# A decode step of two attention and MLP layers on one core: moving K's transposes, the softmax maximum and P's selection in the order of work

## The chip, the core and the metric

The kernel runs on one core of a Trainium2 chip. The metric is the device time of one execution in microseconds (us); lower is better. The core has five engines that run side by side, each through its own instructions in order, and that wait for each other on semaphores: TensorE (PE; its weight loads are shown apart as PEld), VectorE (DVE), ScalarE (ACT), GpSimd (POOL) and SyncE (SP). Here SP issues every load from the chip's memory (HBM) into the on-chip memory; 16 DMA engines carry them out.

## The reference

One token goes through attention, MLP, attention, MLP. Both attentions read the same K and V caches, of which only the last 4096 positions of each of 32 heads count; both MLPs read the same weights.

```python
def _A_ref(x, k_cache, v_cache, wq, wo):          # x (1,1,640), caches (1,32,32768,192)
    B, Sq, D = x.shape
    Hq, Dh = 32, 192
    W = 4096
    q = (x @ wq).reshape(B, Sq, Hq, Dh).transpose(0, 2, 1, 3)
    k = k_cache[:, :, Sk - W:, :]
    v = v_cache[:, :, Sk - W:, :]
    scores = jnp.einsum("bhqd,bhkd->bhqk", q, k) * (Dh ** -0.5)
    p = _softmax(scores, axis=-1)
    o = jnp.einsum("bhqk,bhkd->bhqd", p, v)
    return o.transpose(0, 2, 1, 3).reshape(B, Sq, Hq * Dh) @ wo
...
x = A_x
x = x + _A_ref(_layernorm(x), A_k_cache, A_v_cache, A_wq, A_wo)
x = x + _B_ref(_layernorm(x), B_w1, B_w2, B_w3, B_w4)
x = x + _A_ref(_layernorm(x), A_k_cache, A_v_cache, A_wq, A_wo)
x = x + _B_ref(_layernorm(x), B_w1, B_w2, B_w3, B_w4)
```

With a sequence of one token, the MLP's shifted parts are zero, so that its first half adds nothing and `x + gelu(layernorm(x) @ w3) @ w4` is left. K and V of one head are 4096 x 192 numbers of 2 bytes, 1536 KB each.

## The kernel before

**Loads and cells.** On-chip memory holds 12 cells, each the size of one head's K or V. `take` (L147) hands out the cell that was given back first, `give` returns one. `stream` lists all loads in a fixed order; `need` issues the next ones in that order, on SP's queue. Each issue waits until its cell is free, that is, until the engine that last used it is done; the loads behind it on SP wait too. Issues go through eight DMA semaphores in turn, so that at most eight loads are in flight. In layer 1, heads 0 to 7 have their transposed K still in memory (`NKEEP`), and a few V's stay as well.

**Attention.** Heads go in groups of 4, 8 groups per layer; layer 0 takes the heads from 28..31 down to 0..3, layer 1 up from 0..3. While a group's probabilities are applied to V, the next group's scores are made. The steps, with their lines:

- `T(h, half)`, `transpose_quart` (L433, L450): DVE transposes K of head h in four quarters of 0.94 us each; a half is two. The last quarter gives K's cell back. In most of the kernel the transposed quarters go into an `area` of one cell that is used in turn.
- `S(h, half, ...)`, `scores` (L534): 12 matmuls on PE that add half a head's scores to `ST_ps`.
- Softmax (`softmax_steps`, L551): `part_max` (L557, DVE), `turn_max` (L562, PE), `full_max` (L567 and L572, DVE), `spread_max` (L580 on PE, then the exponential L586 on ACT), `turn_p` (L591, DVE), `swap` (L602 on PE, copy L605 on ACT, sums L607 on PE), `recip` (L614, L616, DVE).
- `pv(h)` (L648): 16 matmuls on PE, P times V; then V's cell is given back and DVE brings the result out (L655). `o_fold` (L657) sums and scales it.
- The group's output product with wo, as a row (`out_row`, L694, added on DVE by `y_ps()`, L702 and L704) or as columns (`out_proj`, L676), and the query of the group after next (`qproj_steps`: L469 or L480, `spread` L494, `repeat` L501, `block` L518).

**Order.** PE, DVE, ACT and SP run in the order in which the code emits their instructions. So the order of the calls in `attention` (L813 to L960) is the order of the work. For a group: first the head h0 and the softmax with the projections between (L850 to L889), then for each of its four heads `pv`, the scores of one more head of the next group, and the fold (L897 to L952). Temporary results of PE share two PSUM buffers (`psm`).

Three kinds of group are told apart. A plain group does this as it stands. The last group but one (`hurry`) has to finish the scores and the softmax of the last group within its own products, since the last group (`final`) has none to make. Before the change, layer 1's last group but one (`quick`) had its own order, in which K's transposes are emitted before the products, and layer 0's another one.

Of the kernel before, what the change touches and what calls it, by code (L numbers as in the profile page):

```python
# [10 lines left out]
F32 = mybir.dt.float32  # L11
# [48 lines left out]
def kernel(  # L60
# [57 lines left out]
    kl = low.tile([P, NKL * Dh], BF16, name="kl")  # L118
# [186 lines left out]
    o_words = o_sb[:].rearrange("p e c i -> p (e c i)")  # L305
# [402 lines left out]
    def turn_row(acc):  # L708
        y_ps = psm.tile([P, ND], F32, tag="psm")
        N = D // 2  # L710
        for n in range(ND):
            a, b = n * P, (n + 1) * P
            for i in range(2):
                lo_, hi = max(a, i * N), min(b, (i + 1) * N)
                if lo_ < hi:
                    nc.tensor.matmul(y_ps[lo_ - a:hi - a, n:n + 1], lhsT=acc[:, lo_ - i * N:hi - i * N],
                                     rhs=ident[0:33, 32 * i:32 * i + 1], start=True, stop=True)
        return y_ps

    def attention(layer, x_cur, rs_cur, x_new, z_new, rs_new, ss_new):  # L720
# [13 lines left out]
        def T(h, half):  # L734
            for q in (2 * half, 2 * half + 1):
                if (h, q) not in Th:
                    Th[h, q] = transpose_quart(layer, h, q)

        def S(h, half, ST_ps, hq):
            if layer == 1 and h < NKEEP:  # L740
                if half == 1:
                    scores(h, [Th.pop((h, q)) for q in range(NT)], 0, ST_ps, hq)
                    give(("T", h))
                return
            scores(h, [Th.pop((h, q)) for q in (2 * half, 2 * half + 1)], 2 * half, ST_ps, hq)
            if half == 1 and layer == 0 and h == last_plain:
                give(("area", layer))
                area[0] = None
# [52 lines left out]
        pending = None  # L801
# [11 lines left out]
        for gi, cur in enumerate(groups):  # L813
            nxt = list(enumerate(groups[gi + 1])) if gi + 1 < len(groups) else []
            hurry = gi + 2 == len(groups)
            final = gi + 1 == len(groups)

            quick = hurry and layer == 1
            ST_n = None
            if nxt:  # L820
                part_max, turn_max, full_max, spread_max, turn_p, swap, recip = softmax_steps(len(cur), ST, sc, o_words)
                ST_n = next_scores()
                if layer == 1 and gi == 0:

                    keep = [hh for hh in nxt if hh[1] < NKEEP]
                    del nxt[:len(keep)]
                    q = qproj_steps(groups[2][0] // QH, xc)
                    q1[2]()
                    q1[3]()
                    for q2, h2 in keep:  # L830
                        for half in range(2):
                            T(h2, half)
                            S(h2, half, ST_n, q2)
                        if q2 == 0:
                            v_words(1)
                    for step in (part_max, turn_max, full_max, spread_max, turn_p):
                        step()

                    need("v", 1, cur[-1] + 1)
                    q[0]()  # L840
                    PT = swap()
                    q[1]()
                    rl = recip()
                    q[2]()
                    q[3]()
                else:
                    if gi == 0:
                        for step in q1:
                            step()
                    h0 = nxt[0][1]  # L850
                    T(h0, 0)
                    part_max()
                    T(h0, 1)
                    S(h0, 0, ST_n, 0)
                    turn_max()
                    full_max()
                    S(h0, 1, ST_n, 0)
                    spread_max()
                    h1 = nxt[1][1]
                    q = None  # L860
                    if gi + 2 < len(groups):
                        q = qproj_steps(groups[gi + 2][0] // QH, xc, row=q_row if gi in rows else None)
                    if q:
                        q[0]()
                    in_row = gi - 1 in rows
                    if pending is not None:
                        y_ps = out_row(layer, *pending, acc, gi - 1 == rows[0]) if in_row else out_proj(layer, pending)
                    turn_p()
                    if quick:
                        y_ps()  # L870
                    T(h1, 0)
                    if q:
                        q[1]()
                        q[2]()
                    if in_row:
                        if not quick:
                            y_ps()
                            if gi - 1 == rows[-1]:
                                add_y(turn_row(acc), 2)
                        pending = None  # L880
                    if pending is not None:
                        add_y(y_ps, 2)
                        pending = None
                    PT = swap()
                    T(h1, 1)
                    if q:
                        q[3]()
                    rl = recip()
                    nxt.pop(0)  # L889
            else:  # L890
                PT, rl = early
            oT = short_bf16("oT", NA, 2)
            fold = None
            order = list(enumerate(cur))
            if layer == 1 and gi == 0:
                order.insert(0, order.pop(cur.index(VC)))
            for hq, h in order:  # L897
                if quick and hq == 1:
                    (q2, h2), (q3, h3) = nxt
                    T(h2, 0)  # L900
                    T(h2, 1)
                elif quick and hq == 2:
                    T(h3, 1)
                pv(layer, h, hq, PT, steps[3] if quick and hq == 3 else fold)
                if final:
                    if hq == 0:
                        add_y(out_proj(layer, pending) if layer == 0 else turn_row(acc), 1)
                    if hq == 1:
                        center_y()
                    fold = None  # L910
                    if hq < QH - 2:
                        o_fold(h, oT, rl)
                    else:
                        def fold(h=h):
                            o_fold(h, oT, rl)

                    continue
                if quick and hq == 1:
                    S(h2, 0, ST_n, q2)
                    S(h2, 1, ST_n, q2)  # L920
                    T(h3, 0)
                elif quick and hq == 2:
                    S(h3, 0, ST_n, q3)
                    o_fold(h, oT, rl)
                    S(h3, 1, ST_n, q3)
                    steps = softmax_steps(len(cur), ST_n, sc, kl[:].bitcast(F32))
                    for step in steps[:3]:
                        step()
                    continue
                elif hurry and hq == 1:  # L930
                    (q2, h2), (q3, h3) = nxt
                    for half in range(2):
                        T(h2, half)
                        S(h2, half, ST_n, q2)
                    T(h3, 0)
                    S(h3, 0, ST_n, q3)
                    T(h3, 1)
                elif hurry and hq == 2:
                    S(h3, 1, ST_n, q3)
                    steps = softmax_steps(len(cur), ST_n, sc, o_words)  # L940
                    steps[0]()
                    steps[1]()
                elif nxt and not (hurry and hq == 3):
                    q2, h2 = nxt.pop(0)
                    for half in range(2):
                        T(h2, half)
                        S(h2, half, ST_n, q2)
                o_fold(h, oT, rl, len(groups) - 4 > gi >= 2 * layer)
                if hurry and hq == 3:
                    for step in steps[4 if quick else 2:5]:  # L950
                        step()
                    early = steps[5](), steps[6]()  # L952
            if final:
                fold()
            if (layer, gi) == (1, 1):
                clear_rows()
            last = (cur[0] // QH, oT)
            if not final:
                pending = last
            ST = ST_n  # L960
# [146 lines left out]
```

## Time and profile before

| | us |
|---|---|
| median of 3 runs | 511.44 (511.27 to 511.87) |
| the profiled execution, its time | 511.84 |
| its span in the profile | 509.9 |
| DVE, transposes of K (L450), 224 of 943 ns | 200.3 busy |
| PE, scores (L534), 1536 | 157.0 busy; 101.6 idle before |
| of that idle time, ended by L450 | 69.1 |
| PE, P times V (L648) | 103.1 busy; 7.4 idle for V's landing |
| DVE, bringing the product out (L655), 64 | 37.2 busy; 110.4 idle before, for PE |
| HBM read | 214.01 MB, 420 GB/s over the span |

All of it is from one profiled execution. In groups of instructions, busy time is that of the engine on that line, and idle time is the time in which the engine had nothing to do just before it; the name behind an arrow is the instruction that ended that time. Windows give, for a stretch of the span, the busy time of each engine, the clock that TensorE was granted, the share of time in which the 16 DMA engines were moving, and GB/s. The timeline gives start and length of instructions, like ones merged, with the idle time before them in brackets. Idle time of an engine that is not the bound costs nothing.

### The profile page before, as it was taken

The page shows a single profiled execution, that of the slowest core. Times are in us where ns is not written, and L with a number is a line of the kernel's source. Part 1 is how long each engine was busy: PE and PEld are TensorE (multiplying, and loading weights), DVE is VectorE, ACT ScalarE, POOL GpSimd, SP SyncE. Part 2 cuts the span into 40 slices and gives each one's busy share as a digit, 9 for nine tenths or more (in the row PEclk, how much of TensorE's full clock was granted, in tenths as well). Part 3 has the DMA queues.
Part 4 walks back from the last instruction along what each step waited for, and adds up shares of the span by engine and source line. Part 5 has one row for each costly group of instructions (what it writes and reads, how often), then busy time and mean ns, then how long its engine had stood idle before and what let it go on. Part 6 is the DMA issues. An engine that isn't in the chain of part 4 may idle for free.

```text
span 509.9 us, 9485 instructions
## 1 busy us (share of the span) xinstructions
PE 328.0 (64%) x4084; PEld 190.0 (37%) x4084; DVE 292.0 (57%) x604; ACT 48.9 (10%) x173; POOL 3.7 (1%) x16
## 2 busy tenths in 40 slices
PE   1057667677586675866665766658656765758685
PEld 0024333333343342533333643435333442434354
DVE  2077557657666656467624244756576566767522
ACT  1000101010010100101010100001010100101111
POOL 2000000000000000000000000000000000000000
PEclk9996666765756667577665585666786577886655
DMA  8999999999999999999999999999999999999996
GB/s 370 432 432 429 438 433 432 429 433 423 419 423 445 432 418 449 428 404 459 429 392 414 377 439 424 435 429 437 429 422 437 432 422 433 426 433 429 419 408 242
DMA packets 12015, 214.63 MB, mean 421 GB/s; under 512 B 2565, under 2 KB 3077, under 8 KB 7429
## 3 DMA queue, kind: packets, MB, share of 16 engines
q1 hardware_dynamic: 11972, 214.02, 98.5%
q8 instruction: 32, 0.52, 0.4%
q14 instruction: 11, 0.08, 0.0%
HBM read 214.01 MB, written 0.00 MB: 420 GB/s over the span
## 4 chain that ended last, share of the span: by engine, by line
DMA 42%; PE 28%; DVE 24%; issue 4%; ACT 1%; SPq 1%; DVEq 0%; ACTq 0%
DMA cell<-in_A_k_cache_dram 24%; DVE cell L450 17%; DMA cell<-in_A_v_cache_dram 14%; PE ST_ps L534 11%; PE O_ps L648 9%; DMA cell<-in_B_w_dram 4%; DVE o_sb L655 2%; PE qr_ps L469 2%; PE nb_ps L580 1%; PE yr_ps L694 1%; DVE words L557 1%; DVE o_sb L591 1%; PE l_ps L607 1%; PE y_ps L1051 1%; PE PT_ps L602 1%
## 5 line engine op out<-in xcount | busy, mean ns | idle before, releaser
L534 PE MATMUL ST_ps<-cell,Qblk 128*16 128x256 bf16 x1536 | 157.0, 364 | 101.6 <-DVE cell L450 69.1
L450 DVE STREAM_TRANSPOSE cell<-cell 128x768 uint32<-128x768 uint32 x224 | 200.3, 943 | 5.8 <-DMA cell<-in_A_k_cache_dram 5.4
L534 PEld LDWEIGHTS <-Qblk 128*16 128x16 bf16 x1536 | 82.8, 108 | 170.8 <-issue 146.9
L648 PE MATMUL O_ps<-cell,PT 128*2 128x384 bf16 x1000 | 103.1, 482 | 9.3 <-DMA cell<-in_A_v_cache_dram 7.4
L655 DVE STREAM_TRANSPOSE o_sb<-O_ps 128x384 f32<-128x384 f32 x64 | 37.2, 581 | 110.4 <-PE O_ps L648 110.3
L648 PEld LDWEIGHTS <-PT 128*2 128x2 bf16 x1024 | 46.1, 102 | 24.7 <-issue 15.7
L591 DVE STREAM_TRANSPOSE o_sb<-o_sb 128x256 bf16<-128x256 bf16 x15 | 6.7, 445 | 33.1 <-ACT o_sb L586 26.1
L663 ACT ACTIVATE words<-oT_ps,words 32x6 bf16<-32x6 f32 x40 | 10.3, 257 | 159.5 <-PE oT_ps L662 148.5
L662 PE MATMUL oT_ps<-o_sb,Lq 128*32 128x6 f32 x160 | 13.8, 195 | 10.4 <-DVE o_sb L655 9.8
L662 PEld LDWEIGHTS oT_ps<-o_sb,Lq 128*32 128x32 f32 x160 | 12.6, 143 | 20.4 <-issue 15.1
L668 ACT ACTIVATE words<-oT_ps,words 32x6 bf16<-32x6 f32 x24 | 6.2, 257 | 111.8 <-PE ST_ps L534 96.3
L480 PE MATMUL qT_ps<-words,wq_sb 128*128 128x1 bf16 x210 | 7.1, 165 | 12.8 <-DMA wq_sb<-in_A_wq_dram 11.9
L694 PE MATMUL yr_ps<-cell,words 128*1 128x320 bf16 x108 | 14.8, 439 | 0.0
L469 PE MATMUL qr_ps<-wq_sb,words 128*1 128x384 bf16 x90 | 14.2, 471 | 0.0
L494 DVE TENSOR_TENSOR o_sb<-qT_ps,words 128x24 bf16<-128x24 f32 (+1 forms) x18 | 3.0, 166 | 18.9 <-PE qT_ps L480 17.1
L480 PEld LDWEIGHTS <-wq_sb 128*128 128x128 bf16 x210 | 6.7, 102 | 14.0 <-DMA wq_sb<-in_A_wq_dram 13.0
L602 PE MATMUL PT_ps<-o_sb,ident 128*32 128x32 bf16 x240 | 6.8, 237 | 7.7 <-DVE o_sb L591 2.6
L607 PE MATMUL l_ps<-o_sb,words 128*128 128x4 f32 x30 | 7.8, 331 | 5.3 <-ACT PT L605 5.3
L602 PEld LDWEIGHTS <-ident 128*32 128x32 bf16 x256 | 5.6, 113 | 14.4 <-issue 14.1
L583 ACT COPY o_sb<-nb_ps 128x1 f32<-128x1 f32 x15 | 2.4, 159 | 88.6 <-PE nb_ps L580 88.6
L667 PE MATMUL oT_ps<-o_sb,Lq 128*32 128x6 f32 x48 | 6.0, 199 | 6.1 <-DVE o_sb L666 6.1
L667 PEld LDWEIGHTS oT_ps<-o_sb,Lq 128*32 128x32 f32 x48 | 5.7, 142 | 10.4 <-issue 9.9
(153 smaller groups left out, 202.0 us busy)
## 6 DMA issues: line engine op xcount, KB each, us to landing
cell<-in_A_k_cache_dram SPq DMA_DIRECT2D x56, 1536.0 KB, 25.6
cell<-in_A_v_cache_dram SPq DMA_DIRECT2D x56, 1536.0 KB, 26.3
cell<-in_A_wo_dram SPq DMA_DIRECT2D x13, 960.0 KB, 23.1
wq_sb<-in_A_wq_dram SPq DMA_DIRECT2D x5, 1536.0 KB, 13.4
cell<-in_A_v_cache_dram SPq DMA_DIRECT2D x6, 768.0 KB, 23.7
cell<-in_B_w_dram SPq DMA_DIRECT2D x1, 1536.0 KB, 11.8
cell<-in_B_w_dram SPq DMA_DIRECT2D x2, 768.0 KB, 10.3
cell<-in_A_wo_dram SPq DMA_DIRECT2D x3, 480.0 KB, 17.0
```

Of the source, the lines that this page charges most:

```text
L450: nc.vector.transpose(Tu, Ku[:, :, q * NY:(q + 1) * NY])
L469: nc.tensor.matmul(qr_ps[32 * i:32 * i + 1, :], lhsT=xc[:, kc:kc + 1], rhs=wq_sb[:, kc, t0 * P + i * N:t0 * P + (i + 1) * N], start=(kc == ...
L480: nc.tensor.matmul(qT_ps[:, tl:tl + 1], lhsT=wq_sb[:, kc, t * P:(t + 1) * P], rhs=xc[:, kc:kc + 1], start=(kc == 0), stop=(kc == ND - 1))
L534: nc.tensor.matmul(ST_ps[r:r + QW, :].rearrange("p (g i) -> p g i", g=ng), lhsT=Q[n], rhs=T4[:, :, f, :, t], start=(hq == 0 and n == 0), s ...
L591: nc.vector.transpose(held["PrT"], held["Pr"])
L602: nc.tensor.matmul(PT_ps[32 * m:32 * (m + 1), :, :, ng * q:ng * (q + 1)], lhsT=Eq[:, q, :], rhs=src[:, m:QW:NM], start=True, stop=True)
L607: nc.tensor.matmul(l_ps[:], lhsT=ones, rhs=held["lh"][:], start=True, stop=True)
L648: nc.tensor.matmul(O_ps[r:r + 2, :], lhsT=PT[:, hq, 2 * i:2 * i + 2], rhs=v_pair(V, h, 2 * i * Dh, 2 * Dh), start=(i < 4), stop=(i >= NB - 4))
L655: nc.vector.transpose(o_sb[:], O_ps.rearrange("p (e a c) -> p e c a", e=2, c=NA))
L662: nc.tensor.matmul(oT_ps[r, :], lhsT=Lq[:], rhs=o_sb[:, e, :, e], start=(e == 0), stop=(e == 1))
L667: nc.tensor.matmul(oT_ps[r, :], lhsT=Lq[:], rhs=o2, start=True, stop=True)
L694: nc.tensor.matmul(yr_ps[32 * i:32 * i + 1, :], lhsT=oT[:, k:k + 1], rhs=wo_t[:, k * D + i * N:k * D + (i + 1) * N], start=(k == 0), stop= ...
```

## The change

The calls in `attention` are put in another order; no step is added or taken out.

- Softmax part of a plain group: `full_max` comes before the transposes of h0's second half, `spread_max` before that half's scores.
- After `turn_p`: the query's `spread`, the output row's addition and P's `swap` come first, the transposes of h1 after `swap`; the query's `repeat` comes after the first half of them.
- The products of a plain group: before the second and the third product (`0 < hq < 3`), the first half of the next head's K is transposed.
- The last group but one in both layers now uses the order that only layer 1's had (`quick`); what stays different by layer goes by `late`, which has the old meaning of `quick`. In layer 0 the first two softmax steps are emitted with the third product, the others after the fourth.

```diff
-            quick = hurry and layer == 1
+            late = hurry and layer == 1
...
                     T(h0, 0)
                     part_max()
-                    T(h0, 1)
                     S(h0, 0, ST_n, 0)
                     turn_max()
                     full_max()
+                    T(h0, 1)
+                    spread_max()
                     S(h0, 1, ST_n, 0)
-                    spread_max()
...
                     turn_p()
-                    if quick:
-                        y_ps()
-                    T(h1, 0)
                     if q:
                         q[1]()
+                    if in_row:
+                        y_ps()
+                    elif pending is not None:
+                        add_y(y_ps, 2)
+                    pending = None
+                    PT = swap()
+                    T(h1, 0)
+                    if in_row and gi - 1 == rows[-1] and not late:
+                        add_y(turn_row(acc), 2)
+                    if q:
                         q[2]()
-                    if in_row:
-                        if not quick:
-                            y_ps()
-                            if gi - 1 == rows[-1]:
-                                add_y(turn_row(acc), 2)
-                        pending = None
-                    if pending is not None:
-                        add_y(y_ps, 2)
-                        pending = None
-                    PT = swap()
                     T(h1, 1)
...
-                if quick and hq == 1:
+                if hurry and hq == 1:
                     (q2, h2), (q3, h3) = nxt
                     T(h2, 0)
                     T(h2, 1)
-                elif quick and hq == 2:
+                elif hurry and hq == 2:
                     T(h3, 1)
-                pv(layer, h, hq, PT, steps[3] if quick and hq == 3 else fold)
+                elif nxt and 0 < hq < 3:
+                    T(nxt[0][1], 0)
+                pv(layer, h, hq, PT, steps[3] if late and hq == 3 else fold)
...
-                if quick and hq == 1:
+                if hurry and hq == 1:
                     S(h2, 0, ST_n, q2)
                     S(h2, 1, ST_n, q2)
                     T(h3, 0)
-                elif quick and hq == 2:
+                elif hurry and hq == 2:
                     S(h3, 0, ST_n, q3)
                     o_fold(h, oT, rl)
                     S(h3, 1, ST_n, q3)
-                    steps = softmax_steps(len(cur), ST_n, sc, kl[:].bitcast(F32))
-                    for step in steps[:3]:
+                    steps = softmax_steps(len(cur), ST_n, sc, kl[:].bitcast(F32) if late else o_words)
+                    for step in steps[:2 + layer]:
                         step()
                     continue
-                elif hurry and hq == 1:
-                    (q2, h2), (q3, h3) = nxt
-                    for half in range(2):
-                        T(h2, half)
-                        S(h2, half, ST_n, q2)
-                    T(h3, 0)
-                    S(h3, 0, ST_n, q3)
-                    T(h3, 1)
-                elif hurry and hq == 2:
-                    S(h3, 1, ST_n, q3)
-                    steps = softmax_steps(len(cur), ST_n, sc, o_words)
-                    steps[0]()
-                    steps[1]()
                 elif nxt and not (hurry and hq == 3):
...
-                    for step in steps[4 if quick else 2:5]:
+                    for step in steps[4 if late else 2:5]:
                         step()
                     early = steps[5](), steps[6]()
```

## The prediction

> **What bounds the kernel now.** I read the page first: the span, the engines, the slices of DMA, the first queue.
>
> ```profile
> span 509.9 us, 9485 instructions
> ...
> PE 328.0 (64%) x4084; PEld 190.0 (37%) x4084; DVE 292.0 (57%) x604; ACT 48.9 (10%) x173; POOL 3.7 (1%) x16
> ...
> DMA  8999999999999999999999999999999999999996
> ...
> q1 hardware_dynamic: 11972, 214.02, 98.5%
> ```
>
> The loads fill 98.5% of the span; no engine passes 64%. Busy time is no bound by itself, so next come windows (busy time by engine, TensorE clock, DMA share, GB/s): the start, two deep stretches, two shallow ones, the seam between the layers.
>
> ```profile
> 0.00:2.00 2.00, 0.29 (x4) 0.18 (x4) 0.06 (x1) 1.26 (x1) 1.45 (x9) 1.00 0.18 31
> ...
> 150.00:180.00 30.00, 20.36 (x214) 10.94 (x210) 18.93 (x35) 3.04 (x10) 0.00 (x0) 0.61 0.99 425
> ...
> 240.00:270.00 30.00, 19.09 (x237) 10.68 (x230) 14.93 (x32) 2.62 (x10) 0.00 (x0) 0.61 0.99 419
> ...
> 280.00:285.00 5.00, 3.21 (x107) 3.12 (x108) 2.58 (x20) 1.66 (x7) 0.00 (x0) 0.50 1.02 384
> 285.00:290.00 5.00, 4.21 (x91) 3.07 (x92) 1.20 (x10) 0.30 (x2) 0.00 (x0) 0.50 1.00 401
> 290.00:295.00 5.00, 4.70 (x133) 3.38 (x129) 0.66 (x4) 0.46 (x2) 0.00 (x0) 0.91 0.93 344
> ...
> 300.00:330.00 30.00, 20.10 (x298) 12.29 (x299) 15.72 (x38) 3.44 (x13) 0.71 (x2) 0.58 1.00 430
> ```
>
> Shares pass 1.00 because packets are counted whole at a window's edges; over some tens of us they even out. Between the start and the end only the seam at 290 to 295 shows a loss, 7% of 5 us, 0.35 us. Then, what SP, which issues every load, waited for, and one load each issued at 160.9 and at 296.4 (the last figure is us from issue to landing).
>
> ```profile
> SPq L55 <- DMA cell<-in_A_k_cache_dram: 21.8, 7, 3.1
> ...
> cell<-in_A_k_cache_dram SPq DMA_DIRECT2D x1, 1536.0 KB, 28.7
> ...
> cell<-in_A_k_cache_dram SPq DMA_DIRECT2D x1, 1536.0 KB, 13.8
> ```
>
> The first line is from 120 to 176 us, where SP waits for earlier landings, not for compute. A 1536 KB load (1.57 MB) at 430 GB/s takes 3.66 us, so 28.7 us is some eight loads in flight and 13.8 us some four. Both depths move 425 to 430 GB/s. The chain of waits (DMA 42%, PE 28%, DVE 24%) runs through compute only because SP's wait for a free cell is on it; the queue behind that wait is not empty. So compute counts only where it frees a cell so late that the queue runs dry. I call cover the time between a load's issue and the landing of the load before it.
>
> **The change, part by part.** No instruction is added or removed, and SP's loads keep their order. Moved are DVE transposes (0.94 us each at L450), small DVE steps, and PE's work between them.
>
> (a) K's next first half ahead of a product. Rows of DVE in a group of layer 0:
>
> ```profile
> 92.20 0.58 DVE L655 STREAM_TRANSPOSE o_sb<-O_ps 128x384 f32<-128x384 f32 x1 [2.16 <-PE O_ps L648]
> 92.71 3.52 DVE L450 STREAM_TRANSPOSE cell<-cell 128x768 uint32<-128x768 uint32 x4
> ...
> 99.00 0.58 DVE L655 STREAM_TRANSPOSE o_sb<-O_ps 128x384 f32<-128x384 f32 x1 [2.73 <-PE O_ps L648]
> ```
>
> DVE idles 2.16 and 2.73 us for the product, then transposes four quarters while PE waits. Two of the four, 1.83 us, now fit into that idle time: 1.8 us less per head, two heads in each of 11 plain groups (6 in layer 0, 5 in layer 1), 40 us along the compute chain. At the end I price it at 0: the loads cover it. If a pair starts late, the evacuation L655 behind it is late by up to 1.8 us.
>
> (b) Full maximum ahead of K's second half. L567 and L572 ran at 110.30 for 0.54 us behind the pair of 108.55 to 110.37; the turned maximum was there at 109.73. They start 0.5 us sooner, L580 no longer queues behind half of the scores (111.79 to about 110.4), and the pair ends about 1.7 us later, at 112.1. The second scores, the q and output rows of L469 and L694 and the cell's release follow that pair.
>
> (c) P's selection early. L450's first pair for the next head (83.04, 1.83 us) moves behind the row add, which ended at 86.30. Both pairs end at 86.30+3.66 = 90.0 instead of 88.18, so that K's cell is free 1.8 us later, with (b) up to 3.5 us. Queued behind it on SP are V's and K's next loads, under covers of 10 us and more (13.8 less one load's 3.66). Price 0; without cover, up to 3.5 us once.
>
> (d) Layer 0's last group but one, the tight place.
>
> ```profile
> 244.10 0.58 DVE L655 STREAM_TRANSPOSE o_sb<-O_ps 128x384 f32<-128x384 f32 x1 [1.29 <-PE O_ps L648]
> 245.74 7.21 DVE L450 STREAM_TRANSPOSE cell<-cell 128x768 uint32<-128x768 uint32 x8 [1.05 <-DMA cell<-in_A_k_cache_dram]
> 254.54 0.58 DVE L655 STREAM_TRANSPOSE o_sb<-O_ps 128x384 f32<-128x384 f32 x1 [1.60 <-PE O_ps L648]
> 255.82 0.42 DVE L557 TENSOR_REDUCE words<-ST_ps 128x1 f32<-128x256 f32 x1 [0.69 <-PE ST_ps L534]
> ```
>
> K of head 2 now gives its cell back before V of head 5 does. V of head 7, issued at 244.10, takes the first cell given back, so it waits for K2's four transposes: they cannot start before the landing at 245.7 and end at 249.3. The load before it lands at about 253.0 (L648 starts on it at 253.04): its cover falls from 8.9 to 3.7 us. The evacuation L655 of 244.10 waits behind the same transposes, 5.25 us; the next product needs V landed at 253.0 anyway, and that hides it. But one half of head 3's scores (1.45 us at L534) now stands behind that product with a fold between: the maximum comes 1.5 to 1.8 us later, and so does the first product of the last group, whose V cell lets the load at 263.63 go. That load goes at about 265.4; the one before it, issued at 257.71, takes 10.8 us and lands at 268.5: cover 4.9 down to 3.1 us.
>
> How much cover does a load need? The trace doesn't show it directly. From below: the first load is issued at 0.74 and the first 2 us carry traffic for 18%, 0.36 us: 2 − 0.36 − 0.74 = 0.9 us. From above: at 281.70 a load goes with the one before it landing at about 285.3 (issued 275.19, 10.1 us), cover 3.6 us, and no share below 1.00 up to 290. I take 0.9, since the start is a direct row: nothing is lost at 3.7 and 3.1 us. At 3.6 the second place loses 0.5 us. A gain from (d) is excluded: it frees no load earlier that the queue waits for. (a) could win back at most the seam's 0.35 us, but the gates there are the mixer's weights, untouched.
>
> At this place a rule bears on the reading itself. The Trainium skill, Perfetto Trace Analysis, Identifying the Most-Contended Engine, calls DMA occupancy misleading with 16 engines and wants HBM utilization. By 435 GB/s, which DMA: Bandwidth & Descriptors, Specifications, gives as the ceiling, an estimate is 430/435 = 99%, so the trace agrees with my reading by share.
>
> **Sum.** Profiled execution 511.84 us (509.9 span, 1.9 around it): (a) 0, (b) 0, (c) 0, (d) 0. It lies 0.40 above the median of the three runs, so against the median: 511.4 us.
>
> **The rivals.**
> 1. Slower: the handover in (d) is not hidden. It decides when the load of 263.63 goes over 4.9 − 0.9 = 4.0 us later. For it: the last group is fed in step with landings, so compute has no head start to spend. Against: the 5.25 us stand in the shadow of V's landing at 253.0. If they were not hidden, delay 1.8 + 5.25 = 7.05 us, loss 3.1 us: 514.5 us.
> 2. Faster: DVE's and PE's accesses slow the loads, and the new order eases it. The best 30 us stretch that isn't edge effect (330 to 360) moves 432 GB/s against 427 to 430 elsewhere: 0.7% of 497 us at most, 3.5 us, so 507.9. Against: 240 to 270 has least DVE time (14.93) and no better rate (419) than 150 to 180 (18.93, 425). The Trainium skill, SBUF — State Buffer, SBUF: two separate sides, holds that engine ports and DMA ports are disjoint; by that rule this rival gives nothing, and the two windows agree. A saving of 40 us on the end would need empty queues, which the shares exclude.
> 3. The change doesn't do what it says: the early transposes wait for the four quarters of their area to be read, and no group gets shorter. In the rows the quarters are read before the product starts (scores end at 90.9, product ends at 92.2). Time all the same 511.4.
>
> **How the numbers follow.** A measurement of this kernel can tell about 0.2%, 1.0 us, from no change. Forecast and rival 3, which share a time: 0.83. Rival 1: 0.11, partial losses above 1.0 us included. Rival 2: 0.06. Range: below, the seam's 0.35 and as much of rival 2: 510.7; above, 0.5 us at each of the two places in (d): 512.4.
>
> **What would show it.** The loads' share stays near 98.5%. Per plain group DVE's idle before L655 shrinks from over 2 us to under 1 and PE's wait for L450 (69.1 us in all) falls by at least a third; the loads in flight get deeper sooner in layer 1. V7's issue moves from 244.1 to about 249.3 and the load of 263.6 to about 265.4. I am wrong if the share between 245 and 275 us falls below 0.97, if the last load lands more than 1 us away from now, or if the rate of full 30 us windows leaves 415 to 440 GB/s.

## The result, and the profile after

The changed kernel is slower: 513.76 us in the median of 6 runs (512.56 to 514.74) against 511.42 us (511.18 to 511.87, 6 runs) for the kernel before on the same chip. The ratio is 1.0045, with a 95% interval of 1.0029 to 1.0061. The forecast was 511.4 us, no change, with a range up to 512.4.

The profiled execution of the changed kernel took 513.16 us, 1.32 us more than that of before (511.84). From its page: the span, the engines, the slices of DMA, the queues (the first carries the loads, the second the code of PE), the summary of the chain of waits, and three groups of instructions.

```profile
span 511.4 us, 9508 instructions
...
PE 302.5 (59%) x4084; PEld 182.1 (36%) x4084; DVE 290.6 (57%) x604; ACT 48.9 (10%) x173; POOL 3.7 (1%) x16
...
DMA  8999999999999999999999999999999999999995
...
q1 hardware_dynamic: 11972, 214.02, 98.3%
q8 instruction: 32, 0.52, 0.4%
...
HBM read 214.01 MB, written 0.00 MB: 418 GB/s over the span
...
DMA 72%; PE 14%; DVE 9%; issue 3%; ACT 1%; SPq 0%; DVEq 0%; ACTq 0%
...
L534 PE MATMUL ST_ps<-cell,Qblk 128*16 128x256 bf16 x1536 | 154.3, 338 | 122.5 <-DVE cell L450 56.2
L450 DVE STREAM_TRANSPOSE cell<-cell 128x768 uint32<-128x768 uint32 x224 | 201.5, 945 | 40.7 <-DMA cell<-in_A_k_cache_dram 38.2
...
L655 DVE STREAM_TRANSPOSE o_sb<-O_ps 128x384 f32<-128x384 f32 x64 | 36.1, 565 | 48.2 <-PE O_ps L648 47.9
```

The compute side did what the change says. DVE no longer idles for the product ahead of L655 (48.2 us instead of 110.4), and the chain of waits is now 72% DMA, 42% before. In exchange DVE waits for K to land (38.2 us): compute has caught up with the loads. The loads themselves fill 98.3% of a span that is 1.5 us longer, with the same bytes. Now the windows of the changed kernel, in the order engines, TensorE clock, DMA share, GB/s:

```profile
30.00:240.00 210.00, 125.44 (x1523) 73.23 (x1525) 131.72 (x240) 18.64 (x63) 0.00 (x0) 0.75 1.00 430
240.00:270.00 30.00, 18.72 (x263) 11.04 (x260) 16.22 (x33) 2.90 (x11) 0.00 (x0) 0.73 0.96 402
245.00:275.00 30.00, 16.38 (x225) 8.60 (x218) 15.13 (x29) 2.63 (x10) 0.00 (x0) 0.73 0.97 403
300.00:330.00 30.00, 21.39 (x310) 13.04 (x311) 16.27 (x40) 3.45 (x13) 0.71 (x2) 0.60 1.01 434
```

Up to 240 us the rate is that of before (430 and 429 GB/s), and from 300 to 480 us both kernels move 431. Only the stretch from 240 to 270 us is worse: 402 GB/s against 419. That is layer 0's last group but one, the place that step (d) of the prediction is about. There, the changed kernel's timeline of DVE (start, length, idle time before in brackets), and behind it that of SP, the load of V of head 7 (V7 below):

```profile
243.78 0.56 DVE L655 STREAM_TRANSPOSE o_sb<-O_ps 128x384 f32<-128x384 f32 x1
245.65 3.56 DVE L450 STREAM_TRANSPOSE cell<-cell 128x768 uint32<-128x768 uint32 x4 [1.31 <-DMA cell<-in_A_k_cache_dram]
249.13 0.54 DVE L655 STREAM_TRANSPOSE o_sb<-O_ps 128x384 f32<-128x384 f32 x1
249.59 3.51 DVE L450 STREAM_TRANSPOSE cell<-cell 128x768 uint32<-128x768 uint32 x4
254.43 0.58 DVE L655 STREAM_TRANSPOSE o_sb<-O_ps 128x384 f32<-128x384 f32 x1 [1.32 <-PE O_ps L648]
256.33 0.42 DVE L557 TENSOR_REDUCE words<-ST_ps 128x1 f32<-128x256 f32 x1 [1.32 <-PE ST_ps L534]
```

```profile
249.23 0.47 SPq L55 DMA_DIRECT2D cell<-in_A_v_cache_dram  x1
```

K of head 2 is transposed until 249.2, and V7, which now takes its cell, is issued at 249.23, 5.13 us later than before (244.10). From 248 to 253 us the first queue's line (packets, MB, share of the 16 engines) reads, in the kernel before and in the changed one:

```profile
q1 hardware_dynamic: 66, 2.11, 98.1%
```

```profile
q1 hardware_dynamic: 56, 1.72, 87.7%
```

So this is where the queue ran dry, though the load ahead of V7 was to land only at 253.0. The single packets show how. Each of the 16 engines moves its part of a load in two 48 KB packets of 1.82 us and then writes a 4-byte mark. In the kernel before, an engine's next packet starts 6 ns after its mark (a mark at 248.917, a packet at 248.923). In the changed kernel, seven engines write their mark for the load ahead between 249.12 and 249.82 us, the first of them before V7 is even issued, and the packets behind come much later (the full-size packets of the other engines are left out):

```
changed kernel, packets by start (us), length (ns), bytes
249.123      9       4
249.172      9       4
249.345      9       4
249.366      9       4
249.579      9       4
249.743      9       4
249.817      9       4
250.511   2146   49152   <- first packet of V7
250.540   2311   49152
250.557   2386   49152
250.596   2442   49152
250.607   2772   49152
```

The first packet of V7 starts 1.28 us after its issue, and these first packets take 2146 to 2772 ns instead of 1821. The engines do not end a load together, as the marks of single loads show (first and last of the 16 engines, as the semaphore's count shows them, 0.37 us after the mark's own packet). Place 1 is V7's load, place 2 the load issued at 263.63 before the change, w4 the MLP load issued at 273.7:

```
us, first/last      V7              place 2         w4              last load       profiled time
before              253.36/256.63   267.95/270.78   280.92/283.74   503.17/506.69   511.84
changed             254.92/256.53   269.45/270.87   282.49/284.90   504.27/508.14   513.16
e2_cell_alone       255.38/256.73   269.61/271.52   282.65/284.88   503.68/507.92   512.94
e8_cell_repaired    253.07/256.78   269.38/271.45   282.46/285.96   504.45/509.21   514.23
e9_both_repaired    253.03/256.51   268.41/271.00   281.73/283.98   502.68/506.65   511.77
e12_both_in_before  254.88/257.02   270.28/272.47   283.24/286.30   505.14/509.64   514.67
```

At V7 the changed kernel's first engine is 1.56 us late and its last one not at all. A mean share over 30 us, or a landing, sees little of that. From w4 on the last engine is late too (+1.16), and at the end by 1.45 us. In all six kernels the time is the last landing plus 5.0 to 5.2 us. Chained end to start into 16 rows, the packets of the first queue also give the time in which an engine carried no load, mean over the 16 (a code packet of the second queue, 0.95 us on one engine, counts as 0.06 here, so that an entry of 0.05 or 0.06 means no idle time):

```
us idle per engine  245 to 255   262 to 268   280 to 290
before                  0.06         0.08         0.45
changed                 0.68         0.05         0.46
e2_cell_alone           0.79         0.06         0.62
e8_cell_repaired        0.06         0.78         0.72
e9_both_repaired        0.06         0.19         0.25
e12_both_in_before      0.87         0.19         0.30
```

### The profile page after: what moved, and what is told of

Its sections match the earlier page's. It is cut to its first block, busy times and chain, and to the rows that moved or that the text cites. A ratio compares the mean times of both kernels' runs of the same rounds, so it can differ in the third digit from the quotient of the medians.

```text
span 511.4 us, 9508 instructions
## 1 busy us (share of the span) xinstructions
PE 302.5 (59%) x4084; PEld 182.1 (36%) x4084; DVE 290.6 (57%) x604; ACT 48.9 (10%) x173; POOL 3.7 (1%) x16
## 3 DMA queue, kind: packets, MB, share of 16 engines
q1 hardware_dynamic: 11972, 214.02, 98.3%
## 4 chain that ended last, share of the span: by engine, by line
DMA 72%; PE 14%; DVE 9%; issue 3%; ACT 1%; SPq 0%; DVEq 0%; ACTq 0%
DMA cell<-in_A_k_cache_dram 47%; DMA cell<-in_A_v_cache_dram 18%; PE ST_ps L534 6%; DVE cell L450 5%; DMA cell<-in_B_w_dram 4%; DMA wq_sb<-in_A_wq_dram 2%; PE O_ps L648 2%; DVE o_sb L655 1%; DVE words L557 1%; ACT o_sb L586 1%; PE y_ps L1036 1%; PE qT_ps L480 1%; PE nb_ps L580 1%; DVE V_ps L637 1%; PE yr_ps L694 1%
## 5 line engine op out<-in xcount | busy, mean ns | idle before, releaser
L534 PE MATMUL ST_ps<-cell,Qblk 128*16 128x256 bf16 x1536 | 154.3, 338 | 122.5 <-DVE cell L450 56.2
L450 DVE STREAM_TRANSPOSE cell<-cell 128x768 uint32<-128x768 uint32 x224 | 201.5, 945 | 40.7 <-DMA cell<-in_A_k_cache_dram 38.2
L534 PEld LDWEIGHTS <-Qblk 128*16 128x16 bf16 x1536 | 84.9, 102 | 181.2 <-issue 155.2
L648 PE MATMUL O_ps<-cell,PT 128*2 128x384 bf16 x1000 | 81.1, 409 | 13.2 <-DMA cell<-in_A_v_cache_dram 13.1
L655 DVE STREAM_TRANSPOSE o_sb<-O_ps 128x384 f32<-128x384 f32 x64 | 36.1, 565 | 48.2 <-PE O_ps L648 47.9
L648 PEld LDWEIGHTS <-PT 128*2 128x2 bf16 x1024 | 36.5, 92 | 26.4 <-issue 17.4
L662 PE MATMUL oT_ps<-o_sb,Lq 128*32 128x6 f32 x160 | 13.2, 191 | 10.9 <-DVE o_sb L655 10.4
L662 PEld LDWEIGHTS oT_ps<-o_sb,Lq 128*32 128x32 f32 x160 | 11.0, 134 | 20.4 <-issue 14.7
L567 DVE TENSOR_REDUCE o_sb<-pmT_ps 1x8 f32<-1x128 f32 x15 | 4.2, 279 | 23.5 <-PE pmT_ps L562 23.0
L469 PE MATMUL qr_ps<-wq_sb,words 128*1 128x384 bf16 x90 | 15.9, 516 | 0.0
L580 PE MATMUL nb_ps<-words,o_sb 1*128 1x1 f32 x30 | 7.9, 329 | 11.6 <-DVE o_sb L572 11.6
L580 PEld LDWEIGHTS nb_ps<-words,o_sb 1*128 1x128 f32 x30 | 7.0, 290 | 15.1 <-issue 12.3
L667 PE MATMUL oT_ps<-o_sb,Lq 128*32 128x6 f32 x48 | 5.1, 179 | 8.2 <-DVE o_sb L666 8.1
```

The source lines that it names most:

```text
L450: nc.vector.transpose(Tu, Ku[:, :, q * NY:(q + 1) * NY])
L469: nc.tensor.matmul(qr_ps[32 * i:32 * i + 1, :], lhsT=xc[:, kc:kc + 1], rhs=wq_sb[:, kc, t0 * P + i * N:t0 * P + (i + 1) * N], start=(kc == ...
L534: nc.tensor.matmul(ST_ps[r:r + QW, :].rearrange("p (g i) -> p g i", g=ng), lhsT=Q[n], rhs=T4[:, :, f, :, t], start=(hq == 0 and n == 0), s ...
L580: nc.tensor.matmul(nb_ps[:], lhsT=held["w"], rhs=one[0:1, :], start=True, stop=True)
L648: nc.tensor.matmul(O_ps[r:r + 2, :], lhsT=PT[:, hq, 2 * i:2 * i + 2], rhs=v_pair(V, h, 2 * i * Dh, 2 * Dh), start=(i < 4), stop=(i >= NB - 4))
L655: nc.vector.transpose(o_sb[:], O_ps.rearrange("p (e a c) -> p e c a", e=2, c=NA))
```

## The experiments

There were twelve runs, of eight new kernels and, again, the changed one, in four groups; each group ran beside the kernel before on one chip. Ratios are to that, with 95% intervals. The first group asks which part of the change costs the time: the cell that V7 gets, the rest of layer 0's last group but one, everything else, or merely where the code lies.

**e1_cell_repaired.** The changed kernel, but K2's cell is given back only after V5's, so that V7 gets V5's cell as before.

```diff
         if q == NT - 1:
-            give(("k", layer, h))
+            if (layer, h) == (0, GROUPS[0][-1][2]):
+                held_back.append(("k", layer, h))
+            else:
+                give(("k", layer, h))
...
             give(("v", layer, h))
+        while held_back:
+            give(held_back.pop())
```

> The changed kernel in its own order on every engine, but K of head 2 gives its cell back after V of head 5, so that V of head 7 is loaded into V5's cell as before. Theory A (V7's load was issued at 249.2 us, when the DMA engines that were ahead had nothing left, and they lost 1 to 2 us each): back to 511.4 +- 0.6 us, no stretched packets near 250 us. Theory B (code loads hit the DMA engines at other times in the new order, wherever V7 goes): stays at 513 to 514.5 us. Theory C (the late first product of layer 0's last group): stays above 512.5 us.

512.79 us (511.36 to 514.69, 12 runs), 1.0020 [1.0008, 1.0033]. V7 is issued at 245.31 and lands as before (253.16/256.64). About half of the loss is gone, half is left: that misses the 511.4 +- 0.6 us of theory A and lies in theory C's band, so the cell is not all of it.

**e2_cell_alone.** The kernel before, with nothing but the cells of two loads exchanged: V7 takes K2's, the next V takes V5's.

```diff
-        i = free.popleft()
+        if key == ("v", 0, 7):
+            free.rotate(-1)
+            i = free.popleft()
+            free.rotate(1)
+        else:
+            i = free.popleft()
```

> The kernel before, its order on every engine untouched, but V of head 7 takes K2's cell and V of head 0 takes V5's. Theory A: V7's load goes at 249.3 us and the time rises by 1 to 3 us, to 512.4 to 514.4. Theories B and C: 511.4 +- 0.5 us, since nothing but one wait is changed.

513.71 us (512.15 to 515.53, 9 runs), 1.0040 [1.0024, 1.0055]: as slow as the whole change, though no instruction is in another place. V7 is issued at 249.70, and the first queue from 248 to 253 us is emptier still:

```profile
q1 hardware_dynamic: 54, 1.57, 81.8%
```

**e3_layer0_old.** The changed kernel, with layer 0's last group but one in its old order; the plain groups, the softmax part and layer 1 stay changed.

```diff
-                if hurry and hq == 1:
+                if late and hq == 1:
                     (q2, h2), (q3, h3) = nxt
...
-                elif nxt and 0 < hq < 3:
+                elif nxt and 0 < hq < 3 and not hurry:
...
+                elif hurry and hq == 1:
+                    (q2, h2), (q3, h3) = nxt
+                    for half in range(2):
+                        T(h2, half)
+                        S(h2, half, ST_n, q2)
+                    T(h3, 0)
+                    S(h3, 0, ST_n, q3)
+                    T(h3, 1)
```

> The changed kernel, with layer 0's last group but one in the order of before (its cells then go as before too); plain groups, softmax part and layer 1 as changed. Theory A: 511.4 +- 0.6 us, the same as with the cell alone repaired. Theory C: 511.4 +- 0.6 too, but then e1 is slower than this by over 1 us. Theory B: 512.5 to 514.5 us.

511.94 us (511.06 to 515.26, 11 runs), 1.0010 [0.9997, 1.0023]: not clear of the kernel before (its one run at 515.26 stays unexplained). No gain and no loss is to be seen from all of the change outside this group; the interval leaves room for a loss of up to 0.2%, and e9 below narrows that.

**e4_before_pad.** The kernel before with 64 more warm-up matmuls at the start, which moves every later instruction of PE in its code.

```diff
-    WARM = 4
+    WARM = 4 + 64
```

> The kernel before with 64 more warming matmuls at the start, while PE waits for its first loads; they shift PE's later code loads by 128 instructions. Theory B: the time moves by 1 us or more, up or down. Theory A: 511.4 to 511.9 us, a small cost at most.

511.69 us (511.40 to 512.35, 11 runs), 1.0005 [0.9996, 1.0013]. This shift, by half a code packet, does not cost the 2 us; other places of the code were not tried.

The second group asks for the half that e1 left: in the changed order, the first half of head 3's scores stands behind the third product and a fold, which can delay the last group's first product, and with it the load at place 2.

**e5_scores_late.** The kernel before, with only that half and the third product's fold moved, in layer 0.

```diff
                     T(h3, 0)
-                    S(h3, 0, ST_n, q3)
                     T(h3, 1)
                 elif hurry and hq == 2:
+                    S(h3, 0, ST_n, q3)
+                    o_fold(h, oT, rl)
                     S(h3, 1, ST_n, q3)
...
+                    continue
```

> The kernel before, with one move alone in layer 0's last group but one: the first half of head 3's scores stands behind the third product and its fold instead of ahead of it. V7's cell and issue stay as they were. Theory D (a second thin place: the load of 263.6 us, let go by the last group's first product, goes 1 to 2 us later and finds engines that have run out): 512.0 to 513.0 us, idle DMA engines near 265 us. Theory A alone (only V7's cell counts): 511.5 +- 0.4 us.

512.07 us (511.54 to 513.32, 11 runs), 1.0003 [0.9995, 1.0012]. On this chip the kernel before was uneven itself (512.08, 511.37 to 514.46), so this says little.

**e6_both_repaired.** The kernel of e1, with that half ahead of the third product again in layer 0.

```diff
                     T(h3, 0)
+                    if not late:
+                        S(h3, 0, ST_n, q3)
                 elif hurry and hq == 2:
-                    S(h3, 0, ST_n, q3)
-                    o_fold(h, oT, rl)
+                    if late:
+                        S(h3, 0, ST_n, q3)
+                        o_fold(h, oT, rl)
                     S(h3, 1, ST_n, q3)
+                    if not late:
+                        o_fold(h, oT, rl)
```

> The changed kernel with both places mended: K2's cell is given back after V5's, and the first half of head 3's scores stands ahead of the third product again in layer 0. All else as changed, the early transposes too. Theory D: 511.5 +- 0.4 us, and no execution above 513. Theory A alone: like e1, 512 to 513.5 us. If the plain groups' new order saves or costs anything at the end, it shows here against the kernel before: by A and D nothing, within 0.2%.

512.28 us (511.40 to 514.21, 11 runs), 1.0005 [0.9991, 1.0019]: no loss to be seen, on the same uneven chip, but two runs above the 513 us named (514.21 and 513.12; the kernel before had three there). So the third group has the three steps of the repair side by side on another chip.

**e7_changed_again, e8_cell_repaired_again, e9_both_repaired_again.** The changed kernel, the kernel of e1 and the kernel of e6, unaltered.

> The changed kernel as it is, so that it stands beside the next two on one chip. All theories: 1.003 to 1.006 of the kernel before.

> The kernel of e1, beside the changed kernel. Theory A: clear of the changed kernel by 1 us or more; 1.000 to 1.002 of the kernel before.

> The kernel of e6, beside the changed kernel and e8. If the second thin place (the load of 263.6 us) costs time of its own beside the changed cell, this is faster than e8 by 0.5 us or more; if not, the two are equal within 0.3 us.

Against 511.50 us (511.27 to 512.31, 30 runs) for the kernel before: e7 512.95 us (512.28 to 514.75, 7 runs), 1.0035 [1.0021, 1.0049]; e8 512.63 us (511.12 to 514.81, 12 runs), 1.0024 [1.0011, 1.0038]; e9 511.71 us (511.21 to 512.75, 11 runs), 1.0003 [0.9994, 1.0011]. With both places mended the loss is gone, and on this chip so is the spread. With the cell alone mended, most of it stays: e8 is 0.32 us below e7, not the 1 us or more of its theory A, and their intervals overlap. From e8 to e9 it is 0.92 us, with intervals that only touch. The timeline of SP at place 2 in e8 and in e9, and then the first queue from 262 to 268 us in e8 and in e9:

```profile
265.27 0.81 SPq L181 DMA_DIRECT2D cell<-in_A_v_cache_dram  x2
```

```profile
263.74 1.90 SPq L181 DMA_DIRECT2D cell<-in_A_v_cache_dram  x4
```

```profile
q1 hardware_dynamic: 117, 1.85, 77.3%
```

```profile
q1 hardware_dynamic: 147, 2.07, 89.0%
```

The load at place 2 goes 1.5 us later in e8, and the engines stand idle for it, at 77.3% against 89.0% (90.0% in the kernel before). The tables above say the same: 0.78 us per engine without a load against 0.19, and e8's first engine at place 2 is 1.43 us behind that of before, while at V7 it was not behind at all.

**e10_fewer_scores.** The kernel before, with most of the score products not made, so that PE runs 2048 instructions fewer. It asks about the engines' drift: is it the loading of PE's code that makes some engines late?

```diff
                 n = 2 * f + t
+                if 0 < n < NCOL - 1:
+                    continue
```

> The kernel before, with two instead of six of the products that make up each half of a head's scores; four are left out, 1024 matmuls and their weight loads, 2048 of PE's instructions, 8 of its 32 code loads. All of HBM's other loads are the same. Theory E (each code load holds up one of 8 DMA engines by some 1.5 us, and the end is set by the engine that is furthest behind): 24 code loads are 3 per engine instead of 4, 1.5 us less, up to 0.7 us more where the seam between the layers no longer runs dry: 509.2 to 510.2 us. Theory F (the code loads cost only their share of the 16 engines' time): 0.13 MB less at 430 GB/s, 0.3 us, with the seam at most 1.0 us: 510.4 to 511.2 us.

510.70 us (510.12 to 512.23, 11 runs), 0.9988 [0.9979, 0.9997]. The second queue of its page, PE's code, is a quarter smaller:

```profile
q1 hardware_dynamic: 11972, 214.02, 98.6%
q8 instruction: 24, 0.39, 0.3%
```

A gain of 0.8 us in the median lies in the smaller of the two expected bands. The profiled execution's last load lands 1.36 us earlier than in the profile before, which would suit the larger one. But w4 lands no earlier (283.82 us, 283.74 before), and 0.87 us of the gain is the shorter way from there to K's first load of layer 1 (4.90 us instead of 5.77), on which scores were left out. What the code loads cost in all stays open.

The fourth group asks whether the two places, put into the kernel before and nothing else, make up the loss.

**e11_scores_late_again, e12_both_in_before.** The kernel of e5 again, and the kernel before with the edits of e2 and e5 together.

> The kernel of e5 (before, with head 3's first half of scores behind the third product), for the chip of e5 gave scattered times to the kernel before too. Theory D: 1.001 to 1.003 of the kernel before, as e8 against e9 shows in the changed kernel. If 1.000 +- 0.001 again, the second place costs time only where the plain groups of the change stand beside it.

> The kernel before with both thin places of the change and nothing else of it: V7 on K2's cell, and the scores behind the product. Theories A and D: the slowdown of the changed kernel or a little more, 1.003 to 1.006. If the two places add up, above e2's 1.004; if the second finds engines that the first has already held up, no more than e2.

Against 511.59 us (511.38 to 512.68, 15 runs): e11 511.86 us (510.95 to 514.32, 11 runs), 1.0009 [0.9995, 1.0022]; e12 514.86 us (514.14 to 515.09, 5 runs), 1.0061 [1.0047, 1.0074]. By itself the late half is not clear of nothing: 1.0009 lies within the 1.000 +- 0.001 under which it costs time only beside the plain groups' new order, just short of theory D's 1.001, and the interval reaches into both. On top of V7's cell it adds some 0.2% (1.0061 against e2's 1.0040, on different chips, with intervals that overlap a little). The load at place 2 goes at 265.00 in e12. The first queue of e12 from 248 to 253 us, and its window from 245 to 275 us:

```profile
q1 hardware_dynamic: 57, 1.77, 86.5%
```

```profile
245.00:275.00 30.00, 16.85 (x201) 8.62 (x200) 14.18 (x28) 2.36 (x9) 0.00 (x0) 0.60 0.95 388
```

388 GB/s instead of 414 in this stretch. No part of the change outside these two places is needed for a loss of the size seen. e12 loses even more than the change itself does, which fits its idle time at the two places: 0.87 + 0.19 us per engine against 0.68 + 0.05.

## Why the prediction was wrong

**The step that failed** is in (d): "I take 0.9, since the start is a direct row: nothing is lost at 3.7 and 3.1 us." Cover was measured to the landing of the load before, and a landing is that of the last engine. At V7 the first of the 16 engines is 3.3 us ahead of the last (253.36 and 256.63 in the kernel before), and an engine is done 0.37 us before its landing is counted, so that a cover of 3.7 us leaves the engines in front nothing. The way from issue to first packet takes 1.28 us here, and 1.03 us at the kernel's start, where the 0.9 came from. So the needed cover was about right for one engine and wrong for a load: it is the lead, the distance between the engines and that lag together, 1.28 + 3.3 + 0.37 = 4.9 us. Over 245 to 255 us an engine stood idle for 0.62 us in the mean (0.68 in the table, less its code packet; nothing in the kernel before), with slower first packets on top. Place 2 fits the rule: e8 has 3.4 us of cover there with the engines of the load ahead 3.8 us apart, and idles; e12 has 3.9 us, but its engines are only 2.0 us apart after V7, and it loses little (0.19).

The Trainium skill, DMA: Bandwidth & Descriptors, Why a DMA increments its semaphore by 16 and not by 1, says that the engines of one DMA finish independently and that the semaphore counts them. The marks agree, 3.3 us apart at V7. That rule speaks against a cover counted to a landing.

**The bound from above** failed with it. The load issued at 281.70 had 3.6 us of cover, and the prediction read a share of 1.00 as no loss. Averaged over the engines and counted in whole packets, such a share does not show engines that run out: by its packets, an engine of the kernel before is without a load for 0.45 us in the mean between 280 and 290 us, 0.12 of it for two code packets, where the two windows showed 1.02 and 1.00. Which load it waits for there is not shown.

**What (d) had right.** V7's issue was forecast at 249.3 and came at 249.23. The evacuation of 244.10 did wait, until 249.13, and V's landing hid that: PE's next product began at 252.93 behind the landing. The maximum came 0.5 us later (256.33 against 255.82), not 1.5 to 1.8, and the load at place 2 at 263.86, not 265.4. In the profiles of the other runs with the late half (e1, e5, e7, e8, e11, e12) it went at 264.55 to 265.27, in those without it at 263.62 to 264.48. So of the two places the profiled execution of the changed kernel lost at V7 only; what the second one costs is seen in the others.

**Rival 1** had the mechanism, a handover in (d) that is not hidden, and nearly the price: 514.5 us against 513.76. Its place and its point were wrong. It was to decide at the load of 263.63, by a delay over 4.0 us; what decided first was V7's load, by a delay of 5.13 us that the prediction had worked out and called covered. That its price came near was luck. A chance of 0.11 was too low: it hung on that one unproved number.

**(a), (b) and (c)** were right at the end. With both places mended (e6, e9), all the rest of the change is worth 1.0005 and 1.0003, within what can be told. Time is saved along the compute chain, though the 40 us themselves were not measured, and it leads nowhere: in layer 1 a load of K is issued at 346.06 instead of 350.07 and simply waits longer in the queue. The same load, from issue to landing, before and after:

```profile
cell<-in_A_k_cache_dram SPq DMA_DIRECT2D x1, 1536.0 KB, 16.0
```

```profile
cell<-in_A_k_cache_dram SPq DMA_DIRECT2D x1, 1536.0 KB, 21.5
```

**Rival 2** (a better rate) is out: before 240 and after 300 us the rates are equal. **Rival 3** is out: in a plain group, the changed kernel's DVE has a pair of quarters ahead of the product's evacuation and no idle time between them.

```profile
94.47 1.84 DVE L450 STREAM_TRANSPOSE cell<-cell 128x768 uint32<-128x768 uint32 x2 [1.95 <-DMA cell<-in_A_k_cache_dram]
96.23 0.54 DVE L655 STREAM_TRANSPOSE o_sb<-O_ps 128x384 f32<-128x384 f32 x1
96.69 1.79 DVE L450 STREAM_TRANSPOSE cell<-cell 128x768 uint32<-128x768 uint32 x2
```

Its 1.95 us of idle time are now for K itself. PE's wait for L450 fell from 69.1 to 56.2 us, by 19% and not by the third that was named; part of the product's wait became a wait for K, which may be why.

**The signs named.** The share stayed at 98.3%, and the rates of full windows in the deep stretches held, as forecast. The last load landed 1.45 us later, beyond the 1 us named, and the share from 245 to 275 us stood at the bound of 0.97. That share was too coarse a test: before it was 0.98. The Trainium skill, Perfetto Trace Analysis, Identifying the Most-Contended Engine, had warned that 16 engines make occupancy misleading; the prediction set the rate in GB/s beside it and took the agreement as proof. But over the whole span the rate only goes from 420 to 418 GB/s. Neither number shows seven engines that stand idle for over a microsecond in the mean.

**How the gap reaches the end.** The mean of a load's 16 marks moves by 0.91 us at the load behind V7 (258.52 before, 259.43 in the changed kernel) and is still 0.87 us later at the last load (505.08 and 505.95). Idle time at V7 (0.62) and longer 48 KB packets between 240 and 300 us (0.32) account for that. The time hangs on the last mark, and the seam between the layers passes that on. There SP's first load of K waits for layer 0's MLP and for layer 1's first query and scores, which wait for w4 to land. From the chain of waits of the changed kernel (start, length, what), with the load that it ends in:

```profile
273.83 11.07 DMA cell<-in_B_w_dram
...
284.95 1.89 PE y_ps L1036 x60
...
287.92 0.94 PE qT_ps L480 x30
...
289.17 1.46 PE ST_ps L534 x19
290.63 0.13 PE Qrep_ps L501
```

```profile
290.67 0.33 SPq L156 DMA_DIRECT2D cell<-in_A_k_cache_dram  x1
```

The same load in the kernel before:

```profile
289.51 0.33 SPq L156 DMA_DIRECT2D cell<-in_A_k_cache_dram  x1
```

In both it goes 5.77 us after w4's last mark (284.90 and 283.74), and in the other four kernels of the table 5.76 to 5.79 us after theirs. The profiled time is that mark plus 227.8 to 228.4 us in all six, while the mark itself moves by 2.6 us. So most of what an execution loses is decided by the last of the 16 engines at w4. The prediction had named these gates and called them untouched.

**What stays open.** How the idle time of the engines in front makes the last one late at w4 was only argued: engines that have lost their lead become the last ones when a code packet holds them up. In the changed kernel the last engine falls 0.8 us behind the others between 280.0 and 284.9 us, with a code packet at 282.0, and in the kernel before, with one at 281.6, it does not; but the records do not name the engines. At the last load the last engine is 2.2 us behind the mean (1.6 before), the other 0.6 us of the profiled loss. Nor was it settled why the times of one kernel scatter: by 2.2 to 4.2 us in the changed kernel, e1, e2, e3, e8 and e11 and by 0.9 us in e12; by 0.7 to 1.8 us in the kernel before, but by 3.1 us on the chip of e5 and e6.

## What to carry to other kernels

In a kernel bound by its loads, ask of every reordering which buffer each load gets, not only when the work is done: giving one load a buffer that came free 5.6 us later cost as much as the whole change (e2). A load needs its issue to come, by its lead, before the first engine of the load ahead runs out, so measure cover to the first mark of the 16 and not to the landing. Here, time saved on engines that wait for the loads bought nothing at the end, and a small loss where the queue was shallow was not won back.

## What the runs showed of the hardware

- **The 16 engines drift apart in one long stream of loads.** Between the first and the last mark of a load lie 2.1 to 2.3 us in the loads issued at 76 to 111 us, 3.2 to 3.3 us at 235 to 268 us and 3.5 us at the end, in the kernel before; in e8 4.8 us at the end. After a place where the queue ran dry, the distance is smaller (1.6 us at V7 in the changed kernel).
- **PE's code comes through the same engines.** The queue of instructions has 32 packets of 16 KB in the changed kernel and 24 in e10, one for each 256 of PE's instructions. In the streams of 48 KB packets each holds up one engine for 0.9 to 1.0 us, and that engine's next packet takes about 2.3 us instead of 1.82, some 1.5 us in all. The Trainium skill, Runtime: NRT & Kernel Launch, Instruction fetch mechanics, tells of 16 KiB blocks of 256 instructions and calls their cost mostly hidden; the count agrees, and the cost seen here falls on the DMA engine that carries the block. Chained into 16 rows from 30 to 241 us, the code packets come on eight rows in turn, the ninth on the row of the first again (in the changed kernel and e9; in the kernel before the twelfth breaks the turn, which may be the chaining). By 241 us that is two packets on four engines, one on four, none on eight; and at the load that lands at 241.99 in the changed kernel, five marks lie within 0.5 us of the last, four are 1.6 to 1.9 us ahead of it and seven 2.7 to 3.3 us. So at this point the drift has the size of the code packets' hold-ups.
- **The lead of a load and its first packets.** From issue to first packet it took 0.96 us (e1, place 2), 1.03 us (kernel's start) and 1.28 us (V7). On engines that had run dry, the first packets took 2146 to 2873 ns instead of 1821.
